# Long convolution and soft-MoE: DFT steps 3 and 1 in two batches of eight units, eight x places, earlier token rows, dispatch weights normalised a round sooner

## Chip, cores and metric

One core of one Trainium2 chip. The metric is the device time of one execution in microseconds (us). The kernel before takes 884.9 us (median of three runs, 883.65 to 887.45).

## What is computed

The reference is a gated long convolution whose result goes through a soft mixture of experts, all in float32:

```python
# x, v: 4 x 11456 x 128
h = np.maximum(pos_emb @ w1, 0.0) @ w2 * np.exp(-0.01 * pos)[:, None]
u = x * v
y = irfft(rfft(u, 2 * S, axis=1) * rfft(h, 2 * S, axis=0)[None], axis=1)[:, :S, :]
t = (x * y).reshape(45824, 128)
logits = t @ phi                        # 32 slots = 8 experts x 4
d = softmax over tokens(logits); c = softmax over slots(logits)
slots = d.T @ t                         # 32 x 128
out = c @ stack(relu(slots[e] @ w1[e]) @ w2[e] for e in range(8))
```

## The kernel before

**The convolution.** The 128 channels go in 8 groups of 16, the channels of a group in 16 units. A transform of length 2S is written as four steps of matrix products on TensorE (PE):

- step 1 (`first` and `p1`, L174): the gated input `x*v` of one unit, prepared by VectorE (DVE) in `p1_sd` (L270, L272, L276, in place in the tile `x`), times a small DFT matrix. 32 matmuls a unit; ScalarE (ACT) copies the two PSUM results of a unit into `T` (L186).
- step 2 (`p2`, L342): 25 products per group over `T`; DVE multiplies each by the filter's spectrum (`m`, L346), GpSimd (POOL) adds the parts into `T` (L352, L353).
- step 3 (`p3`, L362): the inverse on the long axis, 16 matmuls a unit; ACT copies into `E` (L377).
- step 4 (`p4`, L414): the inverse on the short axis, in 7 row blocks; ACT copies half of the result (`vc`, L427), DVE gates it with x (L445, L453), and SyncE (SP) writes the tokens to `scr` in memory.

Round g (g = 1 to 7) works on two groups. First it interleaves step 3 of group g-1 with step 1 of group g: two units of step 1, then step 3 in groups of four units, each followed by the step-1 units whose input is there (2, 4, 4 and 4). Then step 4 of group g-1 is interleaved with step 2 of group g by the table `STEPS`. Round 8 has step 3 and step 4 alone. `inorder` keeps the program's order on an engine.

**Loads around step 1.** SP issues every DMA in program order. The x block of a unit (256 KB, L264) goes into one of six buffers of the pool `ld`; `behind(u)` issues the block of unit u + 6 once unit u has been multiplied, so that the next group's `x_0` and `x_1` follow units 10 and 11. The v block of a unit (224 KB, L254) goes to one of several places; the next group's `v_0` and `v_1` are issued at the end of the step-3/step-1 stage. `spectrum` loads the filter's spectrum for step 2 (nine DMAs of 154 KB, `T<-hs`), 4 ahead of the third batch and 5 ahead of the fourth. `ahead(1)` then prepares units 0 and 1 of the next group on DVE, ahead of step 2's first product in DVE's order; `ahead(2)` loads `x_2` to `x_5` behind the first gate.

**The experts.** The tokens lie in 23 blocks of up to 16 x 128, two blocks to a unit `m` (12 units). `_moe` runs rounds m = 1 to 9 for them: `exps(m)` (ACT, L856), `factor` and the DVE work on the maxima (L846), `softmax(m)` (DVE `mx` L863, POOL L864), `turn` (PE transposes L729, ACT copies L735), `logits(m + 1)` (PE `pl` L802), in some rounds `norm` of an older unit (ACT exponential L870, then five POOL additions L872 to L876 into `csum`), `dispatch(m - 1)` (PE `pa` L897), `collect` (DVE L902). `invert` adds 1e-9 (L907) and takes the reciprocal (L908), `scale` multiplies the combine weights (POOL L930). `norm(m - 3)` stands in rounds 3 to 7, round 2 has `softmax(0)` in its place; unit 5 (`LATE`) is normalised behind the experts' first product. Token rows 0 to 111 of blocks 0 to 5 (the channels of the first seven groups) are loaded from `scr` during round 8, rows 112 to 127 when the last group's gates have written them; blocks 6 and 7 are loaded whole at t = 3 of round 8's step 4, into `xreg` (freed when step 3 is done). Behind the last dispatch come the expert products (L1091, L1111) and then `spread`: 12 output blocks are formed and written (L1148, L1155, `out_dram<-xreg`, 23.5 MB).

Of the kernel before, what the change touches and what calls it, by code (L numbers as in the profile page):

```python
# [62 lines left out]

def conv_part(ctx, tc, cp, moe, xf, vf, xi, xe, pos, w1, w2, win, t1x, t1h, wt, t3, t4, hs, scr):
    nc = tc.nc
    ld = ctx.enter_context(tc.tile_pool(name="ld", bufs=6))
    sm = ctx.enter_context(tc.tile_pool(name="sm", bufs=2))
    hid_ps = ExitStack()
    psh = hid_ps.enter_context(tc.tile_pool(name="psh", bufs=4, space=bass.MemoryType.PSUM))
# [11 lines left out]
    Hs = Tall[:, B * 2 * CG * J :].rearrange("p (k x) -> p k x", k=J)  # L81
    moe.E = cp.tile([128, 4 * C * R + 2 * PW + 2 * EXW], F32, tag="E", name="E")
    E = moe.E[:, : 4 * C * R].rearrange("p (r q c) -> p r q c", q=4, c=C)
    inorder = tc.keep_in_program_order

    RB = 4
# [144 lines left out]
                          in_=ring[:HP, k0 // HK % 2, 1:, :n].rearrange("p g k x -> p g (k x)"))  # L231

    NU = C // 4
    PRE = 2
    HV = 7
    xts, vts = {}, {}

    mts = {}

# [17 lines left out]
    def p1_x(g, u):  # L257
        if g == 0 and u < NU // 2:
            xt = moe.E[:, J * N1 + 8 * RP * u :][:, : 8 * RP].rearrange("p (c q r) -> p c q r", c=2, q=4)
        elif g == 0 and u >= NU - 6:  # L260
            xt = m_half(g, u).rearrange("p (c q r) -> p c q r", c=2, q=4)
        else:
            xt = ld.tile([128, 2, 4, RP], F32, tag="ld", name=f"x_{g}_{u}")
        inorder(nc.sync.dma_start(out=xt, in_=xf[g, u]))  # L264
        xts[u] = xt

# [65 lines left out]
    def p1(g, u, sd, large=False):  # L332
        first_out(g, u, first(g, u, sd, large))
# [151 lines left out]
    for g in range(G + 1):  # L485

        if g == 0:
            for u in range(NU):
                p1(g, u, sds.pop(u))
                if u in (9, 11):  # L490
                    p1_x(1, PRE + 2 + (u - 9) // 2)
                if u in (7, 11):
                    filter_last(u - 7)
        elif g < G:
            if not pso:
                first_ps.close()
                pso.append(conv_ps.enter_context(tc.tile_pool(name="pso", bufs=2, space=bass.MemoryType.PSUM)))
            def third(us, larges):
                for u, large in zip(us, larges):
                    p3(g - 1, u, large)  # L500
                    if u + 2 < NU and u + 2 not in sds:
                        sds[u + 2] = p1_sd(g, u + 2, nc.vector)

            def behind(u):
                w = u + 6
                if w < NU:
                    p1_x(g, w)
                elif w < NU + PRE and g + 1 < G:
                    p1_x(g + 1, w - NU)

            def spectrum(i0, i1):
                for k in range(11 * i0, 11 * i1, 11):
                    inorder(nc.sync.dma_start(out=Hs[:HP, k : k + 11], in_=hs[g - 1, :, k : k + 11]))

            large = g > 1
            ps = [first(g, u, sds[u], not large) for u in range(2)]
            third(range(2), (large, large))
            for u in range(2):
                first_out(g, u, ps[u])
                behind(u)  # L520
            for w in range(PRE + HV, NU):
                p1_v(g, w)
            third(range(2, 4), (large, large))
            for u in range(2, 4):
                p1(g, u, sds[u], not large)
                behind(u)
            for b in range(1, NU // 4):
                if b > 1:
                    spectrum(4 * b - 8, 5 * b - 6)
                us = range(4 * b, 4 * b + 4)  # L530
                third(us, (large, large, not large, not large))
                for u in us:
                    p1(g, u, sds[u], large == (u % 4 < 2))
                    behind(u)
            if g + 1 < G:
                for w in range(PRE):
                    p1_v(g + 1, w)
        else:
            x0, x1, x2 = [sm.tile([128, PW], F32, tag="m", name=f"xl_{i}", bufs=3) for i in range(3)]
            spare = [x0, x1, x2] + [spare[i % 2] for i in (next(turns), next(turns))] + [x0, x2]  # L540
            turns = count()
            xvs = [p4_load(g - 1, rb) for rb in ORDER[:5]]
            moe.weights()
            conv_ps.close()
            moe.logit_banks()
            pso[0] = ctx.enter_context(tc.tile_pool(name="psl", bufs=3, space=bass.MemoryType.PSUM,
                                                    reuse_waits="tile"))
            for u in range(NU):
                p3(g - 1, u)
            moe.places()  # L550
            moe.steps = _moe(moe)
            next(moe.steps)

# [3 lines left out]
        def ahead(step):  # L557
            if nxt_g is None:
                return
            if step == 1:  # L560
                for u in range(PRE):
                    sds[u] = p1_sd(nxt_g, u, nc.vector)
            else:
                for u in range(PRE, PRE + 4):
                    p1_x(nxt_g, u)

        if 0 < g:
# [78 lines left out]
class Moe:  # L646
# [17 lines left out]
    def weights(self):  # L664
        nc = self.tc.nc
        w = self.cp.tile([128, 11 * FF], F32, tag="W", name="ffw")
        extra = self.cp.tile([128, 3 * FF], F32, tag="X", name="extra")
        self.w = w
        aux = self.cp.tile([128, 3 * J], F32, tag="tab1x", name="aux")
        self.phis, self.reps, self.ident = aux[:, :NSLOT], aux[:, NSLOT : NSLOT + 128], aux[:, NSLOT + 128 :][:, :128]  # L670
        self.mask = aux[:, NSLOT + 256 :][:, :4]
        nc.sync.dma_start(out=self.phis, in_=self.phi)
        nc.sync.dma_start(out=self.reps, in_=self.rep)
        self.ring = [w[:, 2 * FF * i : 2 * FF * (i + 1)] for i in range(self.XB)] + [extra[:, : 2 * FF]]
        for i in range(self.XB + 1):
            self.load(i, 0, D - CG)
        for e, place in enumerate((w[:, 10 * FF :], extra[:, 2 * FF :])):
            self.load_weights(e, place)
# [58 lines left out]
    def ahead(self, t):  # L737

        if t == 0:
            make_identity(self.tc.nc, self.ident)  # L740
            self.tc.keep_in_program_order(self.tc.nc.vector.tensor_reduce(
                out=self.mask, in_=self.ident.rearrange("p (a s) -> p a s", a=4), axis=AX.X, op=ALU.add))
        m = B * PW
        if t == 1:
            self.load_tokens(self.w, 0, 2 * m, D - CG, D)
        if t == 2:
            end = 2 * FF * self.XB
            self.load_tokens(self.w[:, 2 * m :], 2 * m, end, D - CG, D)
            self.load(self.XB, D - CG)
        for i in ((), (), (), (6, 7), (8,), (9,), (10,))[t]:  # L750
            self.load(i)


def _moe(mo):
# [31 lines left out]
    xt, xq = mo.xt, mo.xq  # L786
    pls, lts, ets, evs = {}, {}, {}, {}
    pas = {}

    def extent(m):  # L790
        return blocks[units[m][0]][0], sum(blocks[i][1] for i in units[m])
# [75 lines left out]
    def norm(m):  # L867
# [5 lines left out]
        for k in (8, 4, 2):  # L873
            inorder(nc.gpsimd.tensor_tensor(out=h[:, :n, :k], in0=h[:, :n, :k], in1=h[:, :n, k : 2 * k],
                                            op=ALU.add))
        inorder(nc.gpsimd.tensor_tensor(out=csum[:, q0 : q0 + n], in0=h[:, :n, 0], in1=h[:, :n, 1],  # L876
                                        op=ALU.add))

    def turn_weights(m):
        n = extent(m)[1]  # L880
# [23 lines left out]


    def invert(q0, q1):
        inorder(nc.vector.tensor_scalar_add(csum[:, q0:q1], csum[:, q0:q1], 1e-9))  # L907
        inorder(nc.vector.reciprocal(csum[:, q0:q1], csum[:, q0:q1]))  # L908

    def den_sum():  # L910
# [23 lines left out]
    def invert_unit(v):  # L934
        invert(extent(v)[0], sum(extent(v)))
# [5 lines left out]
    def finish(v):  # L941
        invert_unit(v)
        scale_unit(v)

    sizes = [8, 8] + [16] * ((QN - 16) // 16)
    if sum(sizes) < QN:
        sizes.append(QN - sum(sizes))
    starts = [sum(sizes[:m]) for m in range(len(sizes))]
    cts = {}

    def turned(m, pt, early):
# [32 lines left out]
            inorder(nc.tensor.matmul(pas[0], lhsT=reps, rhs=ident, start=True, stop=True))  # L984

    last = NU - 1
    LATE = 5
    yield
    logits(0)
    rd = maxima(0)  # L990
# [25 lines left out]
    for m in range(1, last - 1):  # L1016
        u = units[m]
        exps(m)
        if m > LATE:
            invert_unit(m - LATE - 1)  # L1020
        softmax(m)
        if m > LATE:
            scale_unit(m - LATE - 1)
        turn(u[0])
        fetch(u[0])
        turn_weights(m)
        if m > 1:
            collect(m - 2)
        logits(m + 1)
        rd = spread_max(m + 1)  # L1030
        if m == 2:
            softmax(0)
        elif 2 < m <= LATE + 2:
            norm(m - 3)
        turn(u[1])
        fetch(u[1])
        dispatch(m - 1)
        running_max(m + 1, rd)
        factor(m)
# [1 line left out]
    exps(m)  # L1041
    factor(m)
    collect(m - 2)
    invert_unit(m - LATE - 1)
    softmax(m)
    scale_unit(m - LATE - 1)
    turn(units[m][0])
    fetch(units[m][0])
    logits(last)
# [27 lines left out]
        in_=pst[:, :NSLOT].rearrange("p (e s) -> p e s", s=own)))  # L1077
    share = denominator()
    softmax(last)
    early(1)  # L1080

    FJ = FF // 128
# [32 lines left out]

    up(0)
    up(1)
    norm(LATE)
    turn_hidden(0)
    early(2)  # L1120
    turn_hidden(1)
    finish(LATE)
    norm(LATE + 1)
    for eg in range(2):
        for hf in range(2):
# [190 lines left out]
```

## Time and profile before

| | us |
|---|---|
| median of three runs | 884.9 |
| lowest, highest | 883.65, 887.45 |
| the profiled execution: its time | 887.54 |
| its span | 885.8 |
| mean granted TensorE clock | 0.989 |
| busy: PE, DVE, ACT, POOL | 854.5, 714.0, 453.3, 393.2 |
| seven rounds g = 1 to 7, each | 80.1 to 80.2 |

The profiled execution is one of its own, 2.6 us above the median; every duration below is from it, in us from the start of its span. A row of the timeline names a run of like instructions on one engine, its start, the time from the first start to the last end, and in brackets how long the engine had been idle and what ended that.

### The profile page before, as it was taken

How to read it: one execution, taken by the hardware profiler on the slowest of the kernel's cores; microseconds unless marked ns; L12 is line 12 of the kernel's file. 1: busy time of each engine (PE TensorE's matmuls, PEld its weight loads, DVE VectorE, ACT ScalarE, POOL GpSimd, SP SyncE). 2: the span in 40 equal slices, each digit the busy share in tenths (PEclk: the TensorE clock that was granted, in tenths of full speed). 3: DMA queues.
4: the chain of work that ended last, by engine and by line, in shares of the span. 5: the costliest groups of instructions: out<-in, count | busy, mean ns of one | idle time of the engine just before them, and what ended most of it. 6: DMA issues, size and time to landing. Idle time of an engine off the chain costs nothing.

```text
span 885.8 us, 37579 instructions
## 1 busy us (share of the span) xinstructions
PE 854.5 (96%) x16252; PEld 790.4 (89%) x16252; DVE 714.0 (81%) x1227; ACT 453.3 (51%) x969; POOL 393.2 (44%) x539
## 2 busy tenths in 40 slices
PE   9999999999999999999999999999999999988991
PEld 8998989999999999999999999999999997666540
DVE  5967976898799889988988998899779148884791
ACT  5775558315811851482166128415721637995761
POOL 5003860492088029406910960393079013784850
PEclk9999999999999999999999999999999999999996
DMA  9974674548747755775487476557716878999698
GB/s 315 384 247 130 202 243 157 150 146 262 208 127 221 224 165 150 231 230 167 142 252 200 129 224 212 167 164 237 220 58 194 280 184 270 318 306 320 272 419 372
DMA packets 108338, 197.03 MB, mean 222 GB/s; under 512 B 15881, under 2 KB 71515, under 8 KB 105422
## 3 DMA queue, kind: packets, MB, share of 16 engines
q1 hardware_dynamic: 107854, 194.48, 68.5%
q8 instruction: 128, 2.10, 1.0%
q14 instruction: 36, 0.29, 0.1%
q10 hardware_dynamic: 288, 0.09, 0.0%
q0 software_dynamic: 32, 0.07, 0.0%
HBM read 137.73 MB, written 56.86 MB: 220 GB/s over the span
## 4 chain that ended last, share of the span: by engine, by line
PE 85%; ACT 4%; DMA 3%; DVE 2%; POOL 2%; issue 1%; SPq 1%; DVEq 0%; ACTq 0%; POOLq 0%
PE p L362 23%; PE p L342 20%; PE p L414 16%; PE p L174 10%; PE pw L1148 3%; PE f L196 3%; PE f L208 2%; PE fl L218 2%; PE pa L897 2%; DMA scr<-xl 1%; PE ct L955 1%; PE ph L150 1%; PE pt L729 1%; PE pl L802 1%; ACT xreg L735 1%
## 5 line engine op out<-in xcount | busy, mean ns | idle before, releaser
L352 POOL TENSOR_TENSOR T<-m 111x256 f32<-111x256 f32 (+1 forms) x199 | 151.4, 761 | 340.9 <-DVE m L346 340.9
L346 DVE TENSOR_TENSOR m<-p,T 111x1024 f32<-111x1024 f32 (+1 forms) x175 | 200.2, 1203 | 14.3 <-PE p L342 7.0
L362 PE MATMUL p<-tab,T 111*99 111x112 f32 x2048 | 205.2, 260 | 1.6 <-POOL T L353 0.6
L362 PEld LDWEIGHTS p<-tab,T 111*99 111x99 f32 x2048 | 198.8, 170 | 6.4 <-issue 1.6
L342 PE MATMUL p<-T,W 128*64 128x128 f32 (+1 forms) x3168 | 196.5, 276 | 0.0
L427 ACT ACTIVATE vc<-p 128x412 f32<-128x412 f32 (+1 forms) x112 | 51.6, 513 | 264.9 <-PE p L414 225.5
L342 PEld LDWEIGHTS p<-T,W 128*64 128x64 f32 (+1 forms) x3168 | 181.9, 127 | 1.7
L414 PE MATMUL p<-tab,E 99*64 99x103 f32 (+1 forms) x3584 | 173.8, 252 | 1.2 <-DVE E L375 0.6
L414 PEld LDWEIGHTS p<-tab,E 99*64 99x64 f32 x3584 | 166.1, 136 | 3.3 <-ACT vc L427 0.8
L377 ACT ACTIVATE E<-p 99x448 f32<-99x448 f32 x254 | 131.8, 574 | 64.1 <-PE p L362 62.8
L353 POOL TENSOR_TENSOR T<-m 111x256 f32<-111x256 f32 (+1 forms) x199 | 148.1, 744 | 0.0
L186 ACT ACTIVATE T<-p 128x396 f32<-128x396 f32 x240 | 100.2, 536 | 9.0 <-PE p L174 8.8
L174 PE MATMUL p<-tab1x,x 53*64 53x99 f32 x3648 | 87.5, 246 | 0.3 <-ACT E L224 0.2
L174 PEld LDWEIGHTS p<-tab1x,x 53*64 53x64 f32 x3648 | 80.0, 132 | 5.1 <-ACT E L224 0.7
L445 DVE TENSOR_TENSOR p<-p,vc 128x824 f32<-128x824 f32 (+1 forms) x46 | 46.9, 1019 | 9.1 <-ACT vc L427 9.0
L270 DVE TENSOR_TENSOR x<-x,T 128x448 f32<-128x448 f32 x51 | 31.5, 618 | 22.5 <-PE p L174 11.7
L276 DVE TENSOR_TENSOR x<-T 128x224 f32<-128x224 f32 x102 | 39.2, 425 | 1.8
L272 DVE TENSOR_TENSOR T<-x 128x224 f32<-128x224 f32 x102 | 39.1, 424 | 1.8
L224 ACT ACTIVATE E<-fl 111x512 f32<-111x512 f32 (+1 forms) x50 | 27.1, 625 | 23.0 <-PE fl L218 20.8
L453 DVE TENSOR_TENSOR E<-p,E 128x824 f32<-128x824 f32 x36 | 36.6, 1017 | 1.2
L735 ACT ACTIVATE xreg<-pt 128x512 f32<-128x512 f32 (+1 forms) x68 | 35.0, 612 | 3.6 <-PE pt L729 3.5
L1148 PE MATMUL pw<-cs,so 32*128 32x512 f32 (+2 forms) x192 | 31.7, 609 | 1.3 <-DVE xreg L1155 0.7
(163 smaller groups left out, 962.5 us busy)
## 6 DMA issues: line engine op xcount, KB each, us to landing
x<-in_xf_dram SPq DMA_DIRECT2D x114, 256.0 KB, 4.1
out_dram<-xreg SPq DMA_DIRECT2D x16, 1024.0 KB, 10.4
E<-in_xi_dram SPq DMA_DIRECT2D x37, 412.0 KB, 4.0
T<-in_vf_dram SPq DMA_DIRECT2D x65, 224.0 KB, 5.4
scr<-E SPq DMA_DIRECT2D x67, 206.0 KB, 4.0
T<-hs SPq DMA_DIRECT2D x63, 154.0 KB, 4.5
hs<-E SPq DMA_DIRECT2D x12, 784.0 KB, 4.6
mv<-in_vf_dram SPq DMA_DIRECT2D x42, 224.0 KB, 5.1
```

Of the source, the lines that this page charges most:

```text
L174: inorder(nc.tensor.matmul(ps[h][RP * d : RP * d + RP, i, s, :], lhsT=sd[js, i, s, d, :], rhs=tab1x[js, J * (s + d) : J * (s + d + 1)], st ...
L186: inorder(nc.scalar.activation(dst, src, AF.Copy))
L342: inorder(nc.tensor.matmul(ps[ns, i].rearrange("p b c -> p (b c)"), lhsT=W[:, k0 + i, ns], rhs=Tf[:, :, k0 + i, :], start=True, stop=True, ...
L346: inorder(nc.vector.tensor_mul(m[:, :n].rearrange("p k s e c i -> p k s (e c i)").rearrange("p k s (b c) -> p k s b c", c=CG), ps[:, :n].u ...
L352: inorder(eng.tensor_tensor(out=Ty[:, 0], in0=m[:, :n, 0, 0], in1=m[:, :n, 1, 1], op=ALU.subtract))
L353: inorder(eng.tensor_tensor(out=Ty[:, 1], in0=m[:, :n, 1, 0], in1=m[:, :n, 0, 1], op=ALU.add))
L362: inorder(nc.tensor.matmul(pk[:, i, 2 * s : 2 * s + 2, :].rearrange("p q r -> p (q r)"), lhsT=T[0:N1, s, 2 * k + i, u // 2, :, u % 2], rhs ...
L377: inorder(nc.scalar.activation(dst, src, AF.Copy))
L414: inorder(nc.tensor.matmul(pv[RP * h : RP * h + RP, 2 * k + i, w, j0:], lhsT=E[:J, r, 2 - 2 * w + s, :], rhs=tab4[:, s, o + j0 : o + NJ], ...
L427: inorder(nc.scalar.activation(vc[:, w, :, j0:], pv[:, :, 0, j0:], AF.Copy, scale=2.0 * w - 1.0))
L445: inorder(nc.vector.tensor_tensor(out=pw[:, :, :, j0:], in1=vc[:, :, :, j0:], op=ALU.add, in0=pw[:, 1:2, :, j0:].to_broadcast([128, 2, 4, ...
L1148: inorder(nc.tensor.matmul(po[:, :na].rearrange("p k t -> p (k t)"), lhsT=so[NSLOT * a : NSLOT * a + NSLOT], rhs=ct[NSLOT * a : NSLOT * a ...
```

## The change

- **Order of steps 3 and 1.** Two batches of eight units (`BATCHES`) take the place of the groups of four: units 0 and 1 of step 1, step 3 of units 0 to 7, step 1 of units 2 to 7, step 3 of units 8 to 15, step 1 of units 8 to 15. A table (`wide_banks`) gives each unit its PSUM banks.
- **x places.** `ld` has 4 buffers, and 4 more places lie in `moe.extra` (the memory of the last expert weights, now allocated from the start); they are used in turn. `behind(u)` loads unit u + 8: the next group's `x_0` and `x_1` follow units 8 and 9. `ahead(2)` loads `x_2` to `x_7`. The spectrum's nine loads go together ahead of the second batch.
- **Token rows.** Rows 0 to 111 of blocks 6 and 7 are loaded right behind step 3 of round 8, the last 16 rows at t = 3.
- **Weights of the combination.** Units take turns 1 to 5, 0, 6 to 11. `norm(turns[m - 2])` stands in rounds 2 to 6, `softmax(0)` behind `softmax(last)`, and unit 0 is normalised behind the experts' first product. The addition of 1e-9 moves from DVE to POOL, and `SCALED` says which units a round scales. The output is written in the same order of turns.

```diff
-    ld = ctx.enter_context(tc.tile_pool(name="ld", bufs=6))
+    ld = ctx.enter_context(tc.tile_pool(name="ld", bufs=4))
+    moe.extra = cp.tile([128, 3 * FF], F32, tag="X", name="extra")
+    BATCHES = [range(0, 8), range(8, NU)]
+    XS = 8
-            xt = ld.tile([128, 2, 4, RP], F32, tag="ld", name=f"x_{g}_{u}")
+            n = next(places) % XS
+            if n < 4:
+                xt = moe.extra[:, 8 * RP * n :][:, : 8 * RP].rearrange("p (c q r) -> p c q r", c=2, q=4)
+            else:
+                xt = ld.tile([128, 2, 4, RP], F32, tag="ld", name=f"x_{g}_{u}")
...
-                    if u + 2 < NU and u + 2 not in sds:
-                        sds[u + 2] = p1_sd(g, u + 2, nc.vector)
+                    for w in range(min(u + 3, NU)):
+                        if w not in sds and w in xts:
+                            sds[w] = p1_sd(g, w, nc.vector)
...
-                w = u + 6
+                w = u + XS
...
-            third(range(2, 4), (large, large))
-            for u in range(2, 4):
-                p1(g, u, sds[u], not large)
-                behind(u)
-            for b in range(1, NU // 4):
-                if b > 1:
-                    spectrum(4 * b - 8, 5 * b - 6)
-                us = range(4 * b, 4 * b + 4)
-                third(us, (large, large, not large, not large))
-                for u in us:
-                    p1(g, u, sds[u], large == (u % 4 < 2))
+            for b, us in enumerate(BATCHES):
+                if b:
+                    spectrum(0, 9)
+                us3 = [u for u in us if u >= PRE]
+                third(us3, [wide_banks[3, u] for u in us3])
+                for u in us3:
+                    p1(g, u, sds[u], wide_banks[1, u])
                     behind(u)
...
             moe.places()
+            for i in (6, 7):
+                moe.load(i, 0, D - CG)
...
-                for u in range(PRE, PRE + 4):
+                for u in range(PRE, XS):
                     p1_x(nxt_g, u)
...
-            self.load(i)
+            self.load(i, D - CG if i < 8 else 0)
...
+        inorder(nc.gpsimd.tensor_scalar_add(csum[:, q0 : q0 + n], csum[:, q0 : q0 + n], 1e-9))
...
-        inorder(nc.vector.tensor_scalar_add(csum[:, q0:q1], csum[:, q0:q1], 1e-9))
...
+    turns = list(range(1, LATE + 1)) + [0] + list(range(LATE + 1, NU))
...
+    SCALED = {7: (0,), 8: (1, 2), 9: (3,), 10: (4,)}
...
-        if m == 2:
-            softmax(0)
-        elif 2 < m <= LATE + 2:
-            norm(m - 3)
+        if 1 < m <= LATE + 1:
+            norm(turns[m - 2])
...
     softmax(last)
+    softmax(0)
```

Three places show what moves. First PE, between the end of the second four units of step 3 and the next (round g = 2; `p_1_4` is a bank of step 3 for unit 4 of group 1, `p_2_4` one of step 1 for unit 4 of group 2). Before:

```order
L362 MATMUL p_1_4_3237<-tab_72,T 99x112 x8
L362 MATMUL p_1_5_3253<-tab_72,T 99x112 x8
L362 MATMUL p_1_6_0_3269<-tab_72,T 99x112 x4
L362 MATMUL p_1_6_1_3270<-tab_72,T 99x112 x4
L362 MATMUL p_1_7_0_3286<-tab_72,T 99x112 x4
L362 MATMUL p_1_7_1_3287<-tab_72,T 99x112 x4
L174 MATMUL p_2_4_3303<-tab1x,x_4_2564 64x99 x16
L174 MATMUL p_2_5_3324<-tab1x,x_5_2566 64x99 x16
```

After (line numbers are those of the changed kernel):

```order
L370 MATMUL p_1_10_1_3420<-tab_72,T 99x112 x4
L370 MATMUL p_1_11_0_3436<-tab_72,T 99x112 x4
L370 MATMUL p_1_11_1_3437<-tab_72,T 99x112 x4
L370 MATMUL p_1_12_3453<-tab_72,T 99x112 x8
L370 MATMUL p_1_13_3469<-tab_72,T 99x112 x8
L370 MATMUL p_1_14_0_3485<-tab_72,T 99x112 x4
L370 MATMUL p_1_14_1_3486<-tab_72,T 99x112 x4
L370 MATMUL p_1_15_0_3497<-tab_72,T 99x112 x4
L370 MATMUL p_1_15_1_3498<-tab_72,T 99x112 x4
L175 MATMUL p_2_8_3509<-tab1x,extra 64x99 x16
L175 MATMUL p_2_9_3529<-tab1x,extra 64x99 x16
```

Step 3 now changes to step 1 behind units 7 and 15 alone, where it changed behind units 3, 7, 11 and 15.

Second SP, in the same stage of a round: the loads of x (`in_xf`), of the spectrum (`hs`) and of v (`in_vf`). Before:

```order
L264 DMA x_13_5921<-in_xf_dram 128x512
L513 DMA T<-hs 112x352 x4
L264 DMA x_14_6012<-in_xf_dram 128x512
L264 DMA x_15_6033<-in_xf_dram 128x512
L264 DMA x_0_6055<-in_xf_dram 128x512
L264 DMA x_1_6077<-in_xf_dram 128x512
L513 DMA T<-hs 112x352 x5
L254 DMA v_0_6218<-in_vf_dram 128x448
L254 DMA v_1_6220<-in_vf_dram 128x448
```

After:

```order
L272 DMA x_12_7090<-in_xf_dram 128x512
L272 DMA x_13_7111<-in_xf_dram 128x512
L272 DMA extra<-in_xf_dram 128x512 x2
L522 DMA T<-hs 112x352 x9
L272 DMA extra<-in_xf_dram 128x512 x2
L258 DMA v_0_7444<-in_vf_dram 128x448
L258 DMA v_1_7446<-in_vf_dram 128x448
```

The next group's first two x blocks (the second pair into `extra`) now stand behind all nine loads of the spectrum, directly ahead of `v_0` and `v_1`.

Third SP in round 8, behind step 3. Before:

```order
L683 DMA ffw<-in_mw_dram 128x512 x2
L585 DMA E<-in_xe_dram 128x12
L467 DMA scr<-xl_10643 64x824 x2
...
L388 DMA xl_10645<-in_xi_dram 128x824
L716 DMA xreg<-scr 128x448 x2
L716 DMA xreg<-scr 128x384 x3
```

After:

```order
L696 DMA ffw<-in_mw_dram 128x512 x2
L729 DMA xreg<-scr 112x448 x2
L729 DMA xreg<-scr 112x384 x3
L729 DMA xreg<-scr 112x409
...
L598 DMA E<-in_xe_dram 128x12
L475 DMA scr<-xl_10588 64x824 x2
...
L729 DMA xreg<-scr 16x896
L729 DMA xreg<-scr 16x1152
L729 DMA xreg<-scr 16x2048
```

Ten loads of 112 rows now stand ahead of the first write of the last group's tokens, and three of 16 rows are left where ten of 128 rows stood.

## Rows read from the trace of the kernel before

**Rows 1.** the page, part 4: the chain that ended last, shares of the span

```profile
PE 85%; ACT 4%; DMA 3%; DVE 2%; POOL 2%; issue 1%; SPq 1%; DVEq 0%; ACTq 0%; POOLq 0%
```

**Rows 2.** windows of round g = 5: length, busy PE, PEld, DVE, ACT, POOL, clock, DMA, GB/s

```profile
365.00:445.13 80.13, 80.01 (x1616) 78.66 (x1618) 72.25 (x123) 35.72 (x78) 36.43 (x53) 1.00 0.63 192
404.88:445.13 40.25, 40.25 (x800) 40.12 (x798) 38.67 (x37) 5.53 (x12) 35.77 (x51) 1.00 0.52 157
```

**Rows 3.** timeline of PE, round g = 5

```profile
373.08 1.60 PE L174 MATMUL p<-tab1x,x 53*64 53x99 f32 x64
374.62 6.38 PE L362 MATMUL p<-tab,T 111*99 111x112 f32 x64
380.93 2.98 PE L174 MATMUL p<-tab1x,x 53*64 53x99 f32 x128
...
399.37 2.98 PE L174 MATMUL p<-tab1x,x 53*64 53x99 f32 x128
402.28 1.63 PE L414 MATMUL p<-tab,E 99*64 99x103 f32 x32
403.75 4.74 PE L342 MATMUL p<-T,W 128*64 128x128 f32 x80
```

**Rows 4.** chain of work, round 8: start, us, what ran (count)

```profile
686.84 24.61 PE p L362 x254
```

**Rows 5.** timeline of ACT, end of step 1 in round g = 5

```profile
400.36 3.25 ACT L186 ACTIVATE T<-p 128x396 f32<-128x396 f32 x8 [0.32 <-PE p L174]
```

**Rows 6.** timeline of DVE, round g = 5

```profile
400.73 0.62 DVE L270 TENSOR_TENSOR x<-x,v 128x448 f32<-128x448 f32 x1 [2.08 <-PE p L174]
...
404.88 5.75 DVE L346 TENSOR_TENSOR m<-p,T 111x1024 f32<-111x1024 f32 x5
```

**Rows 7.** timeline of SP, round g = 5

```profile
396.66 2.38 SPq L254 DMA_DIRECT2D v<-in_vf_dram  x2
```

**Rows 8.** DMA issues of 381.8 to 384.4: count, KB each, median us to landing

```profile
x<-in_xf_dram SPq DMA_DIRECT2D x4, 256.0 KB, 2.7
```

**Rows 9.** DMA issues of 396.6 to 399.1

```profile
v<-in_vf_dram SPq DMA_DIRECT2D x2, 224.0 KB, 4.0
```

**Rows 10.** DMA issues of 373 to 376

```profile
mv<-in_vf_dram SPq DMA_DIRECT2D x5, 224.0 KB, 5.8
```

**Rows 11.** chain of work through the expert rounds

```profile
746.93 1.46 ACT et L856 x4
...
752.82 1.10 DVE mx L863
...
754.08 1.45 ACT et L856 x4
...
757.48 0.94 ACT E L870
...
760.52 1.45 ACT et L856 x4
```

**Rows 12.** waits of PE, 736 to 806: us in total, times, longest

```profile
PE pl L802 <- DVE xreg L902: 1.1, 1, 1.1
...
PE pl L802 <- DMA ffw<-scr: 0.5, 1, 0.5
```

**Rows 13.** windows (columns as in rows 2) in round 8, the experts and the writes

```profile
716.00:720.00 4.00, 4.00 (x96) 4.00 (x92) 3.26 (x4) 1.00 (x3) 0.00 (x0) 1.00 0.18 40
780.00:784.00 4.00, 2.84 (x48) 1.25 (x46) 3.93 (x8) 3.74 (x9) 3.69 (x6) 1.00 0.97 315
830.00:880.00 50.00, 36.51 (x230) 16.93 (x228) 34.81 (x62) 29.72 (x55) 23.25 (x36) 0.90 1.01 418
```

**Rows 14.** timeline of SP, round 8

```profile
718.27 1.88 SPq L467 DMA_DIRECT2D scr<-xl  x2
...
733.92 4.71 SPq L716 DMA_DIRECT2D xreg<-scr  x10
```

**Rows 15.** timeline of POOL, behind the experts' first product

```profile
822.59 0.24 POOL L876 TENSOR_TENSOR E<-hs 128x32 f32<-128x32 f32 x1
```

More of the change, by code (lines that the diff above doesn't have):

```diff
@@ L236, in conv_part @@
     xts, vts = {}, {}
+    places = count()
     mts = {}
@@ L489, in conv_part @@
                 p1(g, u, sds.pop(u))
-                if u in (9, 11):
+                if u in (9, 11, 13, 15):
                     p1_x(1, PRE + 2 + (u - 9) // 2)
@@ L515, in conv_part @@
             large = g > 1
+            seq = [(step, u) for us in BATCHES for step in (3, 1) for u in us if step == 3 or u >= PRE]
+            tail = [e for e in seq if e[0] == 1 or e[1] >= 4]
+            wide_banks = {e: (n // 2) % 2 == (1 if large or n >= tail.index((3, NU - 2)) else 0)
+                          for n, e in enumerate(tail)}
+            for u in range(4):
+                wide_banks[3, u] = large
             ps = [first(g, u, sds[u], not large) for u in range(2)]
@@ L666, in weights @@
         w = self.cp.tile([128, 11 * FF], F32, tag="W", name="ffw")
-        extra = self.cp.tile([128, 3 * FF], F32, tag="X", name="extra")
+        extra = self.extra
         self.w = w
@@ L788, in _moe @@
     pas = {}
+    LATE = 5
+    SCALED = {7: (0,), 8: (1, 2), 9: (3,), 10: (4,)}
     def extent(m):
@@ L943, in finish @@
         scale_unit(v)
[L945 to L948, printed above, removed]
+    turns = list(range(1, LATE + 1)) + [0] + list(range(LATE + 1, NU))
+    order = [blocks[i] for v in turns for i in units[v]]
+    order[:1] = [(order[0][0], NB // 2), (order[0][0] + NB // 2, NB // 2)]
+    starts, sizes = zip(*order)
     cts = {}
@@ L986, in _moe @@
     last = NU - 1
-    LATE = 5
     yield
@@ L1019, in _moe @@
         if m > LATE:
-            invert_unit(m - LATE - 1)
+            invert_unit(turns[m - LATE - 1])
         softmax(m)
-        if m > LATE:
-            scale_unit(m - LATE - 1)
+        for i in SCALED.get(m, ()):
+            scale_unit(turns[i])
         turn(u[0])
@@ L1043, in _moe @@
     collect(m - 2)
-    invert_unit(m - LATE - 1)
+    invert_unit(turns[m - LATE - 1])
     softmax(m)
-    scale_unit(m - LATE - 1)
+    for i in SCALED[m]:
+        scale_unit(turns[i])
     turn(units[m][0])
@@ L1117, in _moe @@
     up(1)
-    norm(LATE)
+    norm(turns[LATE])
     turn_hidden(0)
@@ L1121, in _moe @@
     turn_hidden(1)
-    finish(LATE)
+    finish(turns[LATE])
     norm(LATE + 1)
```

## Prediction, made before the changed kernel ran

> **What bounds the kernel now.** I read the chain that ended last first: TensorE holds 85% of it [rows 1], so a saving counts where PE has no wait, and elsewhere only if it frees PE. Then the windows of one round [rows 2]: in 80.13 us PE is busy 80.01, at a granted clock of 1.00. The round can become shorter only if PE needs less time for the same 1616 matmuls. VectorE is close behind: in the second stage, from its first spectral product at 404.88, it is busy 38.67 of 40.25 us. The timeline of PE shows the stage that is re-ordered [rows 3]; there PE goes from one step to the other with no bracketed idle time. Last come the expert rounds, where the chain walks from engine to engine and through DMAs [rows 11], and the writes at the end, at a DMA share of 1.01 and 418 GB/s [rows 13].
>
> **Batches: what a change of step costs.** Two units of step 1 take 374.62 - 373.08 = 1.54 us to the next step, four take 402.28 - 399.37 = 2.91 [rows 3]. Two more units cost 1.37 (0.685 each), so each group has a fixed 1.54 - 1.37 = 0.17. Four units of step 3 (64 matmuls) take 380.93 - 374.62 = 6.31; in round 8, where nothing comes between, 254 take 24.61 [rows 4], or 6.20 for 64. So a group of step 3 has a fixed 0.11. A round has five groups of step 1 and four of step 3, afterwards three and two: 2 x (0.17 + 0.11) = 0.56 us less. This is time in which PE counts as busy, so the cover is PE itself and the gain lies on the path. Bounds: 0, if the fixed parts are something else, and 0.7, the same with a fixed 0.17 for both steps.
>
> What the rows show beside it: weight loads are busy 78.66 us where matmuls are busy 80.01, in the same 80.13 [rows 2], so they run under each other within a step. The Trainium skill ("TensorE: Matmul & The Clock Gate", Part 3) says that a weight load overlaps matmuls in flight only when its row group differs. By that rule step 3, whose weights take 111 rows, could never overlap its loads, and a change of step would cost nothing extra; the sum would then be without the 0.56. This trace speaks against it within step 3.
>
> **Batches: what they add.** ACT's copies of step 1 are slower than PE: eight from 400.36 last 3.25 us [rows 5], 0.41 each and somewhat less by the tail of the last; I take 0.38, 0.76 a unit against PE's 0.685. Four units leave ACT done at 403.61, 0.14 ahead of step 2's first matmul at 403.75, which reads what they write [rows 3, 5]. Four more units in a row add 4 x 0.075 = 0.30 of lag. I take a new wait of 0.2 (0.30 less 0.14, and a handoff); bounds 0 and, at 0.41 a copy, 0.35. The six units of the first batch lag by half of it, and step 3 behind them doesn't read `T`'s new half.
>
> Net of a round: -0.56 + 0.2 = -0.36, times seven rounds **-2.5 us**; bounds -4.9 and +2.5.
>
> **x places.** The extra four places are memory that stood idle. What matters is the next group's start. Step 1's second batch would begin at 402.28 - 0.56 - (8 x 0.685 + 0.17) = 396.1, so units 8 and 9 end at 396.9 and 397.6, and SP can issue `x_0` at 396.9, `x_1` at 397.6, `v_0` at 398.0 and `v_1` at 398.4. Before, the v pair began at 396.66 [rows 7] behind five spectrum loads, and 4.0 was the median to landing [rows 9]; DVE went on at 400.73, and prepared two units until 404.88 [rows 6], 4.15 later. The releaser named there, PE, had long been done with what it names; a v block in flight fits better. Afterwards the nine spectrum loads are issued when unit 7 is done, near 384, and are out of the way. x loads into a quiet queue landed 2.7 after issue [rows 8]. With two x blocks ahead I take 3.0 for `v_0`: 401.0, so step 2's first product starts on DVE at 401.0 + 4.15 = 405.15. Is that late? Step 2 begins on PE at 403.75 - 0.36 = 403.4; five products take 4.74 [rows 3], so the fifth wants its bank, the first's, at about 403.4 + 3.8 = 407.2, and a DVE product takes 5.75/5 = 1.15 [rows 6]. With 0.2 for the handoffs it is in time up to 405.85, that is, for a landing up to 3.7 us after issue. Term: **0**. Upper bound: 5.8 us, as seen with many loads in flight [rows 10]; below nothing, since DVE isn't what PE waits for now. The DVE order is otherwise the same. `ahead(2)` adds two x loads (0.6 each on SP) behind the first gate, and g = 0 two more, both stretches with tens of us until use: 0.
>
> **Expert rounds.** ACT's exponentials start a round. 746.93 to 754.08 is 7.15 us (m = 2), and 754.08 to 760.52 is 6.44 (m = 3) [rows 11]. Round 2 holds `softmax(0)`'s reduction on the chain, 1.10 at 752.82; round 3 instead holds a norm's exponential on ACT, 0.94 at 757.48, and is full on ACT. Moving the reduction out and a norm in makes round 2 like round 3: -0.7. The block loads: `logits` waited 0.5 for a DMA once (m = 6), and 1.1 once (m = 7) in a stretch where PE is busy 2.84 of 4.00 us at a DMA share of 0.97 [rows 12, 13]. The release of the second is put down to DVE, but with the stream full a token load can have been as late. Of ten loads [rows 14], 112/128 of 2.1 MB = 1.84 MB move from the full stretch to 712 to 720, where the share is as low as 0.18 [rows 13]; at 315 GB/s that is 5.8 us of stream. I take 0.4 for m = 6, 1.1 for m = 7 (which also loses its norm), 0.2 for m = 8. Sum of the experts **-2.4 us**. Bounds: -0.7 (round 2 alone), and -0.7 - 5.8 = -6.5 if the rounds followed the stream.
>
> What it costs: ten loads at 4.71 us of issue [rows 14] stand on SP ahead of the first write at 718.27. They can start when step 3 is done, at 686.84 + 24.61 = 711.45 [rows 4], and end at 716.2: 2 us to spare. Three loads of 16 rows (57 to 131 KB) remain, 1.4 us of issue. The Trainium skill ("DMA: Bandwidth & Descriptors", Bandwidth) has transfers under 64 KB mostly overhead and asks for 1 MB; by it a move that makes thirteen DMAs of ten would lose. The bytes are the same and the places where they run are not, so the sum doesn't take that up.
>
> The 1e-9 goes from DVE to POOL: the nearest row of such a size is 0.24 [rows 15]; POOL has that to spare in a round, and in the tail DVE gives back as much. The output's order changes, its bytes don't: the writes stay DMA-bound [rows 13]. 0 for both.
>
> **Sum.** -2.5 - 2.4 = -4.9 to -5. The profiled execution took 887.54, so 882.5; it lies 2.6 above the median of 884.9, which gives **879.9 us**.
>
> **Rivals.**
> 1. *The v load lands late, and step 2 waits each round.* Its point: 3.7 us from issue to landing. For: 4.0 and 5.8 are in the rows [rows 9, 10]. Against: both had many loads in flight, which are gone from that place. At 5.8: 403.8 + 4.15 = 407.95, 2.1 past the point, in six rounds 12.6: 879.9 + 12.6 = **892.5, slower**. At 4.0 it is 0.3 a round, 1.8 in all: 881.7, no change.
> 2. *The change of step is no price, only the ACT lag is new.* For: PE shows no idle time at a change of step. (The Trainium skill's rule above would have it so too.) Against: the 1.54 and 2.91. Then 7 x 0.2 = +1.4 and -2.4: **883.9**, no change.
> 3. *The experts don't follow the stream*: PE's wait of 1.1 was for DVE, as it is put down, and only round 2 gains. -2.5 - 0.7: **881.7**, no change.
> 4. *More comes off*: ACT's lag is hidden (-3.9), and the later rounds gain two thirds of the moved stream (-0.7 - 3.8 = -4.5): **876.5**.
>
> **Chances.** No change is what lies within 0.5% (4.4 us), about what a measurement can tell: 880.5 to 889.3. Forecast 0.42, of which a quarter falls above 880.5; rival 4 0.26; rival 3 0.11; rival 2 0.10; rival 1 0.09, two thirds of it slow; 0.02 for slower ways that aren't listed. Faster: 0.32 + 0.26 = 0.58. Slower: 0.06 + 0.02 = 0.08. Same: the rest, 0.34. The range goes from rival 4 with its bound less 1.5, 875, to 886, which takes in rivals 2 and 3, the milder half of rival 1 and the spread of three runs before; it leaves out the late load and what goes beyond two thirds of the stream.
>
> **What would show it.** In a round of the new profile: step 1 groups of 6 and 8 units, rounds 79.8 apart instead of 80.16; a PE wait of about 0.2 on ACT's L186 ahead of step 2; DVE's first product at 40.2 to 40.3 after the round's start, no wait of PE at step 2's fifth product. In the experts: m = 2 at 6.4, no PE wait for loads in m = 6 and 7. Wrong if the rounds are at or above 80.1 (rivals 1 and 2, told apart by whose wait stands at step 2), or if a PE wait of over 0.5 stays in m = 7 (rival 3).

## The result, and the profile after

The changed kernel takes 894.29 us (median of four runs, 892.37 to 896.08) against 885.39 for the kernel before: 1.0084 times as long, 95% interval 1.0064 to 1.0104. It is slower, outside the range, on the side of the first rival. One execution of a kernel below (E3, 1221.82 us at a granted clock of 0.654, where the others have 0.985 to 0.992) is left out.

| | before | after |
|---|---|---|
| profiled execution | 887.54 | 892.98 |
| span | 885.8 | 891.2 |
| start of round g = 1 | 122.99 | 124.56 |
| rounds g = 1 to 7 | 563.3 | 568.2 |
| end of round 7 to the second exponential of the experts | 54.2 | 54.8 |
| from there to the first output product | 84.1 | 81.9 |
| from there to the end | 61.2 | 61.7 |

The rounds should have become 2.5 us shorter in sum; they became 4.9 longer. The experts became 2.2 shorter (forecast 2.4). The two profiled executions lie 5.4 us apart and the medians 8.9; what fills the rest isn't shown. The start of round 1 varies from 123.0 to 125.3 in the profiles without added products, so its 1.6 isn't put down to the change. These are the rounds g = 2 to 6 in the windows of the changed kernel (length, busy PE, PEld, DVE, ACT, POOL, clock, DMA share, GB/s), which answer to [rows 2]:

```profile
205.69:287.62 81.93, 80.60 (x1614) 78.87 (x1612) 72.08 (x123) 35.64 (x78) 36.47 (x53) 1.00 0.65 191
287.62:369.33 81.71, 80.61 (x1615) 78.85 (x1613) 72.05 (x123) 35.47 (x78) 36.46 (x53) 1.00 0.62 189
369.33:450.10 80.77, 79.75 (x1614) 78.61 (x1612) 72.13 (x123) 35.40 (x78) 36.42 (x53) 1.00 0.63 193
450.10:530.50 80.40, 79.77 (x1614) 78.69 (x1612) 72.04 (x123) 35.50 (x78) 36.38 (x53) 1.00 0.63 192
530.50:612.39 81.89, 80.19 (x1615) 78.84 (x1613) 72.09 (x123) 35.62 (x78) 36.45 (x53) 1.00 0.62 188
```

Before, each of these rounds took 80.16 to 80.17, with PE busy for all but 0.12 in g = 5. (Rounds 1 and 7 of that kernel are longer, 81.58 and 80.89, where the table ahead of the prediction has 80.1 to 80.2 for all seven.) Now PE is idle for 0.6 to 1.7 us in each, and no two rounds are alike. The granted clock is 1.00, its upper level, in all of them. What ended PE's waits between 130 and 692 us (total, times, longest):

```profile
PE p L175 <- issue: 4.0, 8, 1.2
PE p L422 <- issue: 0.9, 1, 0.9
PE p L175 <- ACT T L187: 0.8, 1, 0.8
PE p L350 <- issue: 0.4, 1, 0.4
```

In the kernel before this view has no row between 163 and 685. L175 is step 1, L422 step 4, L350 step 2, and "issue" means that the profile shows nothing that PE waited for. I call such a pause of PE a stop. The timeline of PE in round g = 2, which answers to [rows 3]:

```profile
220.06 2.98 PE L175 MATMUL p<-tab1x,x 53*64 53x99 f32 x128
222.84 0.53 PE L175 MATMUL p<-tab1x,extra 53*64 53x99 f32 x12
223.74 1.42 PE L175 MATMUL p<-tab1x,extra 53*64 53x99 f32 x52 [0.37 <-issue]
225.09 12.52 PE L370 MATMUL p<-tab,T 111*99 111x112 f32 x128
237.54 1.60 PE L175 MATMUL p<-tab1x,extra 53*64 53x99 f32 x64
238.96 2.94 PE L175 MATMUL p<-tab1x,x 53*64 53x99 f32 x128
241.70 0.37 PE L175 MATMUL p<-tab1x,extra 53*64 53x99 f32 x4
242.89 1.59 PE L175 MATMUL p<-tab1x,extra 53*64 53x99 f32 x60 [0.82 <-ACT T L187]
244.41 1.64 PE L422 MATMUL p<-tab,E 99*64 99x103 f32 x32
```

The group of six units takes 5.03 instead of 4.28 and the group of eight 6.87 instead of 5.65, each with one stop in its middle. Step 3's eight units take 12.45 from 225.09 to 237.54, even less than forecast. (Between 220.06 and 223.74 the stop is 0.61 from start to start; the bracket counts from the modelled end of the last matmul.) DVE's row of [rows 6] is here, in round g = 3:

```profile
326.11 0.62 DVE L278 TENSOR_TENSOR extra<-extra,v 128x448 f32<-128x448 f32 x1 [7.09 <-PE p L175]
...
330.10 5.74 DVE L354 TENSOR_TENSOR m<-p,T 111x1024 f32<-111x1024 f32 x5
```

and SP issued the v pair there at

```profile
321.34 0.91 SPq L258 DMA_DIRECT2D v<-in_vf_dram  x2
```

so DVE could go on 4.8 after that issue began, past the 3.7 us that the first rival names. The first spectral product started 2.6 us behind PE's first product of step 2, and that part of the round took 41.84 in place of 41.32.

### The profile page after: what moved, and what is told of

It reads as the page before. It is cut to its first block, busy times and chain, and to the rows that moved or that the text cites. A ratio compares the mean times of both kernels' runs of the same rounds, so it can differ in the third digit from the quotient of the medians.

```text
span 891.2 us, 37540 instructions
## 1 busy us (share of the span) xinstructions
PE 856.9 (96%) x16252; PEld 792.1 (89%) x16252; DVE 708.1 (79%) x1215; ACT 452.2 (51%) x969; POOL 396.7 (45%) x551
## 5 line engine op out<-in xcount | busy, mean ns | idle before, releaser
L370 PE MATMUL p<-tab,T 111*99 111x112 f32 x2048 | 201.9, 260 | 1.6 <-POOL T L361 0.6
L350 PE MATMUL p<-T,W 128*64 128x128 f32 (+1 forms) x3168 | 196.4, 276 | 0.5 <-issue 0.4
L350 PEld LDWEIGHTS p<-T,W 128*64 128x64 f32 (+1 forms) x3168 | 181.2, 127 | 3.4 <-DVE m L354 1.0
L422 PE MATMUL p<-tab,E 99*64 99x103 f32 (+1 forms) x3584 | 173.0, 252 | 1.5 <-issue 0.9
L422 PEld LDWEIGHTS p<-tab,E 99*64 99x64 f32 x3584 | 165.1, 136 | 3.6 <-issue 1.9
L175 PE MATMUL p<-tab1x,extra 53*64 53x99 f32 x1856 | 49.3, 247 | 4.3 <-issue 3.2
L175 PEld LDWEIGHTS p<-tab1x,extra 53*64 53x64 f32 x1856 | 43.2, 132 | 7.9 <-issue 4.4
L278 DVE TENSOR_TENSOR extra<-extra,v 128x448 f32<-128x448 f32 x21 | 13.0, 621 | 41.3 <-DMA v<-in_vf_dram 21.2
L175 PE MATMUL p<-tab1x,x 53*64 53x99 f32 x1792 | 42.1, 245 | 0.8 <-issue 0.8
L175 PEld LDWEIGHTS p<-tab1x,x 53*64 53x64 f32 x1792 | 39.6, 132 | 1.9 <-issue 1.2
```

Of the source, the lines that this page charges most:

```text
L175: inorder(nc.tensor.matmul(ps[h][RP * d : RP * d + RP, i, s, :], lhsT=sd[js, i, s, d, :], rhs=tab1x[js, J * (s + d) : J * (s + d + 1)], st ...
L350: inorder(nc.tensor.matmul(ps[ns, i].rearrange("p b c -> p (b c)"), lhsT=W[:, k0 + i, ns], rhs=Tf[:, :, k0 + i, :], start=True, stop=True, ...
L370: inorder(nc.tensor.matmul(pk[:, i, 2 * s : 2 * s + 2, :].rearrange("p q r -> p (q r)"), lhsT=T[0:N1, s, 2 * k + i, u // 2, :, u % 2], rhs ...
L422: inorder(nc.tensor.matmul(pv[RP * h : RP * h + RP, 2 * k + i, w, j0:], lhsT=E[:J, r, 2 - 2 * w + s, :], rhs=tab4[:, s, o + j0 : o + NJ], ...
```

## Experiments

Two theories. **A:** PE runs out of instructions in a long group of step 1. **B:** the new places and the order of the loads make step 2 late (the first rival). The page has two rows that bear on A. Of the changed kernel, part 1 (busy us, share, instructions) and a queue of part 3 (packets, MB, share), by which instructions come in by DMA:

```profile
PE 856.9 (96%) x16252; PEld 792.1 (89%) x16252; DVE 708.1 (79%) x1215; ACT 452.2 (51%) x969; POOL 396.7 (45%) x551
...
q8 instruction: 128, 2.10, 1.0%
```

16252 / 128 is 127 matmuls to a packet of 16 KB. Step 1 runs 32 matmuls in 0.685 us, 127 in 2.7; step 3 takes 12 for 127. Counted from the start of the program, the stops of the changed kernel's rounds stand behind matmuls 2762, 2888, 4032, 4408, 5678, 6054, 7700, 9220, 10490, 10866 and 12512. The distances 376, 1270, 1646 and 4812 are 3, 10, 13 and 38 times 125.3 to 127.

The trace tells more than these counts. PE's 32868 instructions (with weight loads and its sequencer's 364) over 128 packets are some 257 a packet, and counted so, the eleven stops lie whole multiples of 256 apart (one is off by one). So each stands at the end of a packet. The DMA records say when the next packet came in (the first on record is matched with the third 256 instructions, and so on in order). For the stop at 242.89 this is the instruction queue's row in the view of the DMA queues from 239.5 to 239.8:

```profile
q8 instruction: 1, 0.02, 34.4%
```

34.4% of 16 engines over 0.3 us is 1.65 for this one packet, where the median of all is 1.0; it lies from 239.64 to 241.29, and PE goes on 1.60 after its end. At all eleven stops PE goes on 1.27 to 1.60 after the end of the packet that holds its next instruction, and in none of the twelve profiles does it take up a packet less than 1.07 after that packet's end. So these stops are waits for instructions.

**E1, groups of four again**, all else of the change kept:

```diff
-    BATCHES = [range(0, 8), range(8, NU)]
+    BATCHES = [range(b, b + 4) for b in range(0, NU, 4)]
...
-                if b:
-                    spectrum(0, 9)
+                if b > 1:
+                    spectrum(4 * b - 8, 5 * b - 6)
```

With the groups, the spectrum's loads go back to two parts; E3 keeps them together.

> The changed kernel with steps 3 and 1 in groups of four units again; the eight x places, the early token rows and the earlier norms stay. Theory A (PE runs out of instructions inside a long group of step 1, the waits named issue): no issue wait inside step 1, rounds of 80.2 us as before, and the experts' 2.3 us saved: 885.4 - 2.3 = 883. Theory B (the new places and the later loads of x and v make step 2 late): the rounds stay at 80.6 to 81.9 and the time is above 888.

887.25 us, 1.0003 times the kernel before (0.9983 to 1.0022; before in the same session 886.94). The loss is gone, so it hung on the long groups (or the order of loads that came with them) and not on the places. The forecast of 883 is missed: the experts' gain doesn't show. Four rounds of g = 1 to 7 take 80.17 to 80.33, and three have stops that lengthen a group by 0.9, 0.4 and 0.6, behind matmuls 5677, 7699 and 12135. At the first two the changed kernel stops too; the work there is the same in both, so E1 can't tell the end of a packet from the unit that runs there (E5 can).

**E2, the experts' part alone** (the changed class `Moe` and `_moe`, the two early loads, the convolution as before).

> The kernel before with the experts' part of the change alone (early token rows, norms a round sooner, order of turns). Both theories: rounds of 80.2, exponentials 6.43 to 6.45 apart in rounds 2 to 8, 885.4 - 2.3 = 883. If the experts' gain of the changed kernel came from its later start, 885.

888.15 us, 1.0016 (1.0000 to 1.0031): missed by 5. Its rounds of exponentials are 6.44 as expected. Three rounds of the convolution were late at step 2 in that profile (80.5, 80.6, 80.9).

**E3, the batches split**: the last unit of step 3 moves into the batch's step 1.

```diff
+            for us in BATCHES:
+                e = (3, us[-1])
+                seq.remove(e)
+                seq.insert(seq.index((1, us[3])) + 1, e)
...
```

> The changed kernel with the last unit of step 3 of each batch put inside the batch's step 1, so that three or four units of step 1 follow each other where there were six and eight; every load is issued behind the same unit as in the changed kernel. It gives back the two changes of step (0.56 us a round). Theory A: the issue waits in step 1 go or fall below 0.3 a round, rounds of 80.2 to 80.5, about 884. Theory B: first spectral product of step 2 as late as in the changed kernel, rounds of 80.8 or more, 890 or more.

889.18 us (nine executions), 1.0024 (1.0010 to 1.0039). The place that stopped is now smooth; PE's timeline of E3 in round g = 2:

```profile
234.99 1.60 PE L175 MATMUL p<-tab1x,extra 53*64 53x99 f32 x64
236.40 1.56 PE L175 MATMUL p<-tab1x,x 53*64 53x99 f32 x64
237.89 1.78 PE L370 MATMUL p<-tab,T 111*99 111x112 f32 x16
239.60 1.60 PE L175 MATMUL p<-tab1x,x 53*64 53x99 f32 x64
241.03 1.55 PE L175 MATMUL p<-tab1x,extra 53*64 53x99 f32 x64
242.51 1.63 PE L422 MATMUL p<-tab,E 99*64 99x103 f32 x32
```

Eight units and one of step 3 in 7.52, as the sum of their parts. Of 4.9 us of loss in the rounds of the changed kernel 0.4 is left in E3 (124.00 to 687.73, 563.7, against 563.3 before); two rounds are still longer than expected, 80.6 and 80.8. The expected 884 is missed by 5, as in E2, and the experts' gain doesn't show.

**E4, the loads beside step 1 left out**: for g = 2 to 7 POOL sets the late x and v blocks to zero.

```diff
-        inorder(nc.sync.dma_start(out=xt, in_=xf[g, u]))
+        if g > 1 and (u < PRE or u >= XS):
+            inorder(nc.gpsimd.memset(xt, 0.0))
+        else:
+            inorder(nc.sync.dma_start(out=xt, in_=xf[g, u]))
...
```

> The changed kernel, groups g = 2 to 7, with the x blocks of units 8 to 15, 0 and 1 and the v blocks of units 9 to 15, 0 and 1 set to zero by POOL in place of being loaded: the transfers that run beside step 1's batches are gone (the output is then that of other inputs). Theory A with contention (the fetch of instructions is late because the loads fill the DMA engines): no issue wait over 0.2 in step 1, rounds of 79.6 to 79.9, about 882. Theory A without contention (the fetch is too slow for eight units in a row whatever else runs): the waits of 0.5 to 1.5 stay, rounds of 80.4 to 81. Theory B: step 2 in time, and rounds shorter by 0.5 at most in two of them.

885.74 us in one execution (before 886.94). Its timeline of PE at the same place of round g = 2:

```profile
235.19 1.61 PE L175 MATMUL p<-tab1x,extra 53*64 53x99 f32 x64
236.61 2.95 PE L175 MATMUL p<-tab1x,x 53*64 53x99 f32 x128
239.35 1.76 PE L175 MATMUL p<-tab1x,extra 53*64 53x99 f32 x64
241.04 1.63 PE L428 MATMUL p<-tab,E 99*64 99x103 f32 x32
242.62 0.56 PE L356 MATMUL p<-T,W 128*64 128x128 f32 x6
```

The eight units take 5.86 instead of 6.87; over g = 2 to 6 they take 5.67 to 5.86 (changed kernel 5.67 to 7.27), the groups of six 4.29 to 4.58 (4.29 to 5.04). So most of the stops in long groups hang on the transfers beside them. Where a packet and the next both begin in step 1, their first matmuls lie 2.7 to 2.9 us apart here in rounds 2 to 6, close to PE's own 2.7; in the changed kernel 3.1 to 4.2 in nine cases of eleven; in the kernel before, with step 3 in between, 7.8. Two things miss: stops of 1.4 in round 7's group of six and of 0.8 in round 4's step 4 are left, and the rounds are 79.95 to 80.46, not 79.6 to 79.9. Around the first run loads that E4 leaves in (DMA share 0.46 from 621 to 625). Around the second runs nothing: the DMA share is 0.00 from 397 to 399.5, and the packet, alone up to 400.8, still begins 1.2 behind the first matmul of the packet before. So transfers aren't needed for a stop. Step 4 to step 2 takes 1.58 here instead of 1.47, and step 2 begins 0.05 after the end of ACT's copy: the ACT lag that the prediction added, 0.1 to 0.25 in rounds 2, 3, 5 and 6.

**E5, the program shifted** by 64 matmuls, work unchanged:

```diff
     idle_products(6)
+    t = psh.tile([128, 128], F32, tag="ph", name="shift")
+    for _ in range(32):
+        inorder(nc.tensor.matmul(t[:32, :16], lhsT=zero[:, :32], rhs=zero[:, :16], start=True, stop=True))
```

> The changed kernel with 32 small products of zeros ahead of its first product on PE (64 matmul records, 3 to 4 us at the start at most). Everything behind them has the same order, but each instruction stands 64 matmuls further on in PE's program. Theory A, that PE stops at ends of fixed stretches of its program (the waits of five kernels stand behind the same counted matmuls, 4032, 5678, 7700, 9220, 10490, a multiple of some 125 apart, whatever runs there): the waits come 64 matmuls earlier in the work. In the groups of six units of step 1 (192 matmuls) no end but one near matmul 76, with half of step 3 ahead of it, so 4.29 us in every round in place of 5.04, 4.88 and 5.01; in the groups of eight a wait near matmul 132 and one right behind the group, not near 196 to 240. Theory B (a wait for a PSUM bank or a copy whose release isn't recorded): waits at the same units as before the shift.

896.61 us, 1.0129 (1.0102 to 1.0157), of which the products are 3.6. In round g = 2 the stop has left step 1 for step 4:

```profile
244.85 1.59 PE L175 MATMUL p<-tab1x,extra 53*64 53x99 f32 x64
246.37 0.39 PE L425 MATMUL p<-tab,E 99*64 99x103 f32 x2
248.22 1.49 PE L425 MATMUL p<-tab,E 99*64 99x103 f32 x29 [1.45 <-issue]
```

The stops are at counts 2888, 4158, 4534, 6054, 6181, 7700, 8970, 9346, 10992 and 12512, those of the unshifted kernel or whole packets from them, so 64 matmuls earlier in the work. The groups of six take 4.29 in rounds 2, 3, 4, 6 and 7 (4.53 and 4.74 in the others). In the groups of eight the stop is not near 132 in each round but at 166, 200 and 234 in rounds 3, 4 and 5, in round 6 behind the group (12 matmuls into step 4) and in round 7 at 176: a round has 1612 matmuls and thirteen packets 1646, so the ends drift by 34 a round, which the expectation had left out. At all ten PE goes on 1.07 to 1.49 after the end of a packet. The theory B of this expectation, a wait for a PSUM bank or a copy, would have kept the same units; it is excluded.

**E6, groups of four with the same shift.**

> The first experiment's kernel (groups of four, all else of the change) with the same 32 products ahead. Theory A: the ends of stretches fall in step 1's groups at matmul 45 in place of 109, with more of step 3 around them, so the rounds are 80.17 us each and the waits of 0.9, 0.4 and 0.6 that three rounds of that experiment show are gone; in the experts the waits move by 64 matmuls, for better or worse. The time follows the waits: 884 to 888, that of the first experiment less 0 to 2, plus what the products cost. Theory B: the same three rounds wait as before the shift.

889.56 us, 1.0039 (1.0022 to 1.0055) with the 3.6 us of products. No round stops in step 1, as expected. One stop of 0.46 is left in step 4 of round 2. In the experts of that profile one round took 9.99 (a wait of 2.0 ahead of a product of logits, put down to DVE and not at the end of a packet). The shift didn't make the kernel faster.

**E7, the convolution's part alone** (`ld`, `BATCHES`, `XS` and what goes with them; `Moe` and `_moe` as before).

> The kernel before with the convolution's part of the change alone: batches of eight, eight x places, the loads' order. Theory A: the whole loss lies here, rounds of 80.4 to 82 with waits in the groups of six and eight, 886.9 + 7.4 + 2 = 896 if the experts' part is a gain of 2, 894 if that part is worth nothing in the median, as the second experiment has it. If the loss came from both parts together (the memory shared by x places and weights), below 890.

893.65 us, 1.0090 (1.0064 to 1.0116): the whole loss. Its stops named issue or ACT stand at ten of the changed kernel's eleven counts (not at 9220). Step 2 is late in rounds 2 to 5 of this profile: steps 2 and 4 take 0.4, 0.4, 0.9 and 0.8 more than 41.32. That is theory B beside theory A.

**E8, the kernel before, second profile.**

> The kernel before once more, for a second profile. Theory A: waits named issue behind the same counted matmuls as in the first profile (12133, 15412, 15665), of other lengths; rounds of 80.17 apart from them. It shows how far one profile lies from the next: 885 to 889.

885.94 us. Rounds 2 to 6 take 80.16 to 80.26. Of the three named counts 15664 stops again (0.6), 12133 by at most 0.2 and 15412 not, so an end is a place where PE may stop, not one where it must. It stops by 1.0 at another end (15791). From the second exponential to the first output product it takes 81.6, where the first profile had 84.1.

**E9, the first v block early**: ahead of the spectrum's loads.

```diff
                 if b:
+                    if g + 1 < G:
+                        p1_v(g + 1, 0)
                     spectrum(0, 9)
...
-                for w in range(PRE):
+                for w in range(1, PRE):
                     p1_v(g + 1, w)
```

> The changed kernel with the next group's first v block issued ahead of the spectrum's loads, some 13 us sooner (its place is free by then); its x blocks stay where they are. The prediction's slower rival: with that block there, DVE starts step 2 at the landing of the x block, about 1 us sooner, so its first product lies at most 1.7 us behind PE's in every round, step 2 and 4 take 41.3 in all of them (41.74 and 41.84 in two rounds of the changed kernel), and 0.5 to 1.5 us come off: 892.5 to 893.5. Theory A alone (waits inside step 1): those stay, the groups of eight at 5.7 to 7.3, and the time stays above 891.

891.21 us, 1.0057 (1.0032 to 1.0082). DVE in round g = 3:

```profile
319.82 0.63 DVE L278 TENSOR_TENSOR extra<-extra,v 128x448 f32<-128x448 f32 x1 [4.05 <-PE p L175]
...
325.80 5.75 DVE L354 TENSOR_TENSOR m<-p,T 111x1024 f32<-111x1024 f32 x5 [0.47 <-PE p L350]
```

DVE now waits for PE ahead of its first product. Steps 2 and 4 take 41.32 to 41.39 in rounds 1 to 4 and 6, and 42.19 in round 5, which also stops at an end inside step 2. The stops in step 1 stay (2.6 us in five, and 0.8). The intervals of this kernel and the changed one overlap, so the 2 to 3 us between them aren't settled by the times; the trace shows 0.9 us of it (0.4 and 0.5 in the changed kernel's rounds 2 and 3).

**E10, the experts' part, second profile.**

> The second experiment's kernel for a second profile. There step 2 was late on DVE in three rounds (first product 1.7 to 2.9 behind PE's, rounds of 80.5 to 80.9), in code that this kernel shares with the kernel before. If that is chance, other rounds or none show it; if the experts' part brings it about, the same rounds do. From the second exponential to the first output product 80 to 82.5, as in seven profiles with this part.

888.62 us. Step 2 is late again in two or three rounds (first product 2.1 to 2.5 behind PE's in rounds 1, 3 and 4), but in others than in E2, except round 3. Whether that is chance isn't settled.

## Why the prediction was wrong

**The step that failed** is "Batches: what they add", and with it "Net of a round". The change of step has the price that the prediction read: the stage of steps 3 and 1 takes 36.88 in round g = 4, where step 1 has no stop, against 37.38: -0.50, forecast -0.56. Step 1's groups give 0.30 of it and step 3's 0.20. The rule of the Trainium skill weighed there ("TensorE: Matmul & The Clock Gate", Part 3), from which the prediction drew that a change would cost nothing, doesn't fit this stage. But against that gain the sum set ACT's lag alone and took any further unit of step 1 at 0.685; that PE's own instructions could be late stood in it at nothing, without a reason. They were: they come in packets of some 127 matmuls, step 1 uses one up in 2.7 us, and with the loads of x and v in flight the next was often not there. A group of four with step 3 on both sides passes one end; eight pass two, 2.7 us apart. The stops cost 0.6 to 2.4 us in rounds 2, 3, 5, 6 and 7, and 1.1 in round 4, there in step 4. On average a round came out 0.7 us longer (4.9 in seven) and not 0.36 shorter. E7 puts the loss in the convolution, E1 and E3 in the long groups, E4 in the transfers beside them, E5 at ends of the program's packets, and the DMA records show the packets late. Why a packet is late is less clear: E4 says that most of it goes with other transfers and that one stop needs none, and the records don't say what held a packet up.

**The first rival** came in part. Its point (3.7 us from issue to landing) was passed in rounds 2 and 3, by 0.4 and 0.5 us of wait, not by 2.1 in six rounds; in E7 four rounds lost 2.5 to it. `v_0` lands 3.0 to 4.7 after its issue in the four rounds where the trace has the landing, and in round 3 DVE goes on 4.8 after it; 5.8 isn't reached. That the 892.5 of this rival is near the result is luck: its mechanism gives 0.9 of 4.9.

**ACT's lag** (+0.2) is there in E4, 0.1 to 0.25; in the changed kernel step 4 to step 2 takes 1.47 as before (but for the stop in round 4), with ACT done 0.3 to 0.9 ahead of step 2: PE's stops give it the time. (The sum's upper bound should read 0.40: 4 x 0.135 less 0.14.)

**Experts, -2.4**: 2.2 in the two first profiles. The rounds of exponentials, answering to [rows 11]:

```profile
754.06 1.45 ACT et L872 x4
755.51 1.95 ACT xreg L748 x4
757.46 0.95 ACT E L886
758.40 1.95 ACT xreg L748 x4
...
760.50 1.45 ACT et L872 x4
```

Round 2 has become 6.43 long and full on ACT, as forecast, and rounds 6 and 7 too, without a wait for loads (a later round still waits 0.5 for one). Yet the median doesn't get it (E2). Over all profiles the stretch from the second exponential to the first output product takes 84.1, 81.6 and 81.7 with the old experts (kernel before twice, E7), and 79.8 to 83.2, on average 81.7, with the new ones (after, E1 to E6, E9, E10): 0.8 less. The outputs then take 61.5 to 62.0 where they took 61.2 to 61.3, 0.4 more. So the term is worth -0.4 and not -2.4. What failed is the price of the waits, 1.7 of the 2.4. The largest, 1.1 us in round 7 [rows 12], was taken for a late token load. The trace has it end with DVE's `collect`, the releaser that the view names and the third rival took:

```profile
782.91 0.31 DVE L902 SCALAR_TENSOR_TENSOR xreg<-xreg,pa 128x128 f32<-128x128 f32 x1
783.27 1.06 PE L802 MATMUL pl<-xreg,aux 128*32 128x512 f32 x8 [1.12 <-DVE xreg L902]
```

The second profile has no such wait, so the first was chance; it isn't the end of a packet either, which comes 12 matmuls later. Nor did the early token rows end the waits for loads: at the same product E3 waits 0.4 and E4 0.7 for one. The 0.8 that is left of the gain is close to the 0.7 of round 2 alone, as the third rival has it.

**The rest** held: with the ten early loads the stretch from round 7 to the second exponential takes 54.2 to 54.8 in eight profiles against 54.2 (55.8 in E2, where a product of logits waited 1.5), and the added POOL operation doesn't show. The range was missed because neither the sum nor a rival had an engine wait for its own instructions.

## What to carry to other kernels

Count instructions per microsecond, not only busy time, when short matmuls are put in a row: here 47 matmuls (with their weight loads 93 instructions) per us outran the supply where more than some 127 stood together with loads in flight, and breaking the row with slow matmuls cost less than the stops. A pause that the view of waits calls "issue" can be held against the records of the instruction queue. A wait that one profile shows may be chance: take a second profile before its removal goes into a sum. None of the variants that compute the same is faster than the kernel before.

## What wasn't expected of the hardware

PE stops at the same counted matmuls in kernels that do different work there (2888 is step 2 in the changed kernel and step 1 in E5, 7700 step 4 and step 1), for 0.2 to 1.9 us, and shifting the program by 64 matmuls shifts the stops by 64 in the work (E5). One of them is put down to ACT in the view of waits (0.82 at 242.89), at a count that fits the others, 1.60 after the end of a packet. The executions of one kernel differ by 3.5 to 7.6 us where such stops fall in the rounds, but by 3.8 to 8.6 in the kernel before as well, so that spread isn't shown to come from them.
